# An mLSTM and Fourier-mixing kernel on Trainium2: first MLP weights by pairs of column blocks, and another order of VectorE's queue in the later batches

## The chip, the core and the metric

The kernel runs on one core of a Trainium2 chip. A core has TensorE (PE in the profile; PEld are its weight loads), VectorE (DVE), ScalarE (ACT), GpSimd (POOL) and SyncE (SP), each with an instruction queue that is worked off in order. Here SP's queue issues the transfers. The metric is the device time of one launch in microseconds.

## What is computed

Four batches, each of 768 tokens with 8 heads of 40 features, so 320 columns. First an mLSTM cell, then a block of Fourier mixing and an MLP:

```python
# mLSTM, per token t (the kernel works in chunks of 128 tokens instead)
C = f_stab * C + i_stab * outer(v_t, k_t);  n = f_stab * n + i_stab * k_t
y[t] = sigmoid(o_t) * (C @ q_t) / max(|n . q_t|, 1)

# Fourier mixing and MLP, x of shape (4, 768, 320)
mixed = real(fft(fft(x, axis=1), axis=2))
u = x + mixed
un = (u - mean(u)) / sqrt(var(u) + 1e-06)
out = u + relu(un @ w_ch1) @ w_ch2        # 320 -> 1280 -> 320
```

## The kernel before

**One order for everything.** No scheduler moves instructions. `at(slot, phase, fn, ...)` puts a call into a plan, and `run` executes the plan sorted by slot and, in a slot, by phase: EVAC 0, FILL 1, MAIN 2, FILL_PE 3, with fractions between. The order of these calls is the order of each engine's queue. Each batch has an mLSTM of six chunks, a mixing stage and 32 MLP slots: batches 0 to 3 have their MLP in slots 31 to 62, 63 to 94, 95 to 126 and 127 to 158. In the MLP slots of one batch the mLSTM and the mixing of the next are interleaved, so TensorE's queue alternates between the two. Slot 31 begins at 59.3 us, slot 51 at 124.0.

**mLSTM.** For each chunk TensorE makes scores (L465), VectorE multiplies them with the decay matrix W (L471), GpSimd masks W (`affine_select`, L443), scales q (qg, L431) and v (vw, L437) and decays the state (L455). L479 multiplies qg with the state, L486 multiplies W with v. VectorE divides (L544 to L550) and adds state updates (L515). GpSimd's L521 copies a small column.

**Mixing.** `mix_fold` (L606 to L618, mostly VectorE) folds pairs of token chunks. In batches 2 and 3 `mix_fold_again` (L635 to L645, VectorE and GpSimd) folds once more. Products into PSUM banks `pz` and `pu` follow. `mix_add` (L746 to L757) adds a chunk of `pu` to x on VectorE, in place, and takes mean and variance. For chunk c=3 it first copies a row within `pu` (L746) and clears another (L747). ScalarE centers (L765, `uc`), TensorE transposes (`mix_turn`, L772, into a bank `put`) and ScalarE copies the result to `uT` (L777). `ORDER` = (0, 5, 1, 4, 2, 3) is the order of the chunks. `mix_rstd` takes 1/sqrt of the variances of six chunks, a 128x6 tile: four steps L785 to L790 for a start value, and three Newton iterations of three steps, L792 to L794, all on VectorE.

**PSUM.** Four banks pm0 to pm3 serve the mixing and the MLP. In batches 2 and 3 the mixing has its banks written out: `MIX` (L593) gives `pu` the banks 3, 2, 2 for the pairs (0,5), (1,4), (2,3), and `put` the banks 3, 3, 3, 3, 2, 3 for the chunks of ORDER.

**MLP.** Batch 0 uses plain products: `mlp_in` (L836, with the 64 rows of the tail on L840) and `mlp_out` (L942). Batches 1 to 3 use a Strassen-Winograd form of seven products instead of eight. `mlp_block` computes two blocks of 128 hidden columns in four slots, five times: products L896, tails L901, copies of banks on ScalarE (L914, L918, L923), and `add` (L905) on VectorE, which adds a bank to a hidden block and so frees that bank. `mlp_out_pair` computes the output of two chunks in four slots, three times, over two banks x and y in turn: product L998, then `residual` (L948) on VectorE, which reads the bank before the next product may go into it. `hidden_sums` (L984, VectorE) forms the sums that the next pair needs.

**Weights.** `w_ch1` and `w_ch2` reach the kernel as 64-bit floats. A `Piece` of 128x640 numbers (640 KB) is loaded (`load`, SP), then `take` (VectorE, L344 and L346) splits off exponent and mantissa, `convert` (ScalarE, L351 and L352) turns them into floats, and `join` (VectorE, L358, L360, L364) puts the value together. There are five pieces for `w_ch1` and five for `w_ch2`, with two raw buffers between them. `w1_sb` holds rows 0 to 127 and 192 to 319 of `w_ch1`, each with all 1280 columns; `w1t_sb` holds the 64 rows between. `weight_sums` (L874) forms the sums of blocks of `w1_sb` for the Winograd form; the letters A11, A21, A12, A22 stand for row part and column block.

Of the kernel before, what the change touches and what calls it, by code (L numbers as in the profile page):

```python
# [10 lines left out]
FP = mybir.dt.float32  # L11
# [39 lines left out]
def kernel(  # L51
# [51 lines left out]
    h_first = const.tile([L, NP, 1], FP, name="h_first")  # L103
    w1_sb = const.tile([L, 2, DFF], FP, name="w1_sb")
    w1t_sb = const.tile([L, DFF // 2], FP, name="w1t_sb")
    w2_sb = const.tile([L, NFF, DM], FP, name="w2_sb")
# [33 lines left out]
    def gates(gp):  # L140
# [41 lines left out]
        mlstm_load(0, 2)  # L182
        w1_pieces[1].load()
        for t in hT_bufs + Cd_bufs:
# [135 lines left out]
    class Piece:  # L320
# [33 lines left out]
        def join(self):  # L354
# [7 lines left out]
            for d in self.dst:  # L362
# [3 lines left out]

    part = 2 * DM
    w1_pieces = [Piece([w1_sb[:, f // 2, f % 2 * part:(f % 2 + 1) * part]], w_ch1[:, f * part:(f + 1) * part])
                 for f in (0, 2, 1, 3)]
    w1_pieces.insert(2, Piece([w1t_sb], w_ch1[:, 4 * part:]))  # L370
    w2_flat = w_ch2.rearrange("p f m -> p (f m)")
# [407 lines left out]
    def mix_rstd(b):  # L779

        k = mixes[b]
        v = st_p.tile([L, NT], FP, name="v", tag="v")
        y = k.rstd = st_p.tile([L, NT], FP, name="rstd", tag="rstd")
        t = st_p.tile([L, NT], FP, name="t", tag="t")
        nc.vector.tensor_scalar(out=v, in0=k.u[:, :, DM + 1], scalar1=1e-6, scalar2=None, op0=OP.add)  # L785
        nc.vector.tensor_scalar(out=t.bitcast(U32), in0=v.bitcast(U32), scalar1=1, scalar2=None,
                                op0=OP.logical_shift_right)
        nc.vector.tensor_scalar(out=y.bitcast(U32), in0=t.bitcast(U32), scalar1=-1.0, scalar2=float(0x5F3759DF),
                                op0=OP.mult, op1=OP.add)
        nc.vector.tensor_scalar(out=v, in0=v, scalar1=-0.5, scalar2=None, op0=OP.mult)  # L790
        for _ in range(3):
            nc.vector.tensor_tensor(out=t, in0=y, in1=y, op=OP.mult)  # L792
            nc.vector.tensor_tensor(out=t, in0=t, in1=v, op=OP.mult)
            nc.vector.scalar_tensor_tensor(out=y, in0=t, scalar=1.5, in1=y, op0=OP.add, op1=OP.mult)  # L794

    def plan_mix(b, s0, x_done, s_feat, s_add, s_turn):
        for j in range(TG):
            p = TG - 1 - j
            at(x_done[j], FILL + 0.5, mix_fold, b, p)
            if b == 0:  # L800
                at((s0 - 4, s0 - 2, s0)[j], FILL_PE + 4, mix_seq, b, p, (0, 1))
                at((s0 - 2, s0 - 2, s0)[j], FILL_PE + 4, mix_tail, b, p)
            elif b == 1 or j == 0:
                if b > 1:
                    for step, slot in enumerate((x_done[0], x_done[-1] + 2, x_done[-1] + 6)):
                        at(slot, FILL + 0.55, mix_fold_again, b, step)
                at(s0, FILL_PE + 4, mix_seq, b, p, (0,))
                at(s0 + 1, FILL_PE + 4, mix_seq, b, p, (1,))
                at(s0 + 2, FILL_PE + 4, mix_tail, b, p)
# [5 lines left out]
        for c, a, t in zip(ORDER, s_add, s_turn):  # L815
            at(a, FILL, mix_add, b, c)
            at(t, FILL + 0.1, mix_center, b, c)
            at(t, FILL_PE + (5 if b == 0 or c in ORDER[:4] else -0.1), mix_turn, b, c)
            if b > 0:
                at(t, FILL_PE + 6, mix_turn_out, b, c)  # L820
            elif t < s_mlp:
                at(t + 1, FILL + 0.2, mix_turn_out, b, c)
            else:
                at(t + 1, EVAC, mix_turn_out, b, c)


    def mlp_in(b, gr, f):
# [6 lines left out]
        for i, ch in ((1, 1),) if f % 2 else ((0, 0), (0, 1), (1, 0)):  # L834
            f0 = (f // 2 * 2 + i) * L
            nc.tensor.matmul(k.pm[i], w1_sb[:, ch, f0:f0 + L], u[2 * ch], start=(ch == 0), stop=False)  # L836
        if f % 2:
            for i in range(2):
                r = slice(i * TAIL, (i + 1) * TAIL)
                nc.tensor.matmul(k.pm[i], w1t_sb[r, f // 2 * L:(f // 2 + 1) * L], u[1][r], start=False, stop=True)  # L840

# [17 lines left out]
    def weight_sums(n):  # L859

        w = w1_sb.rearrange("p c (n two t) -> p c two n t", two=2, t=L)
        if n == 0:
# [5 lines left out]
        def view(t):  # L868
            return t.rearrange("p (n t) -> p n t", t=L)

        S2, S3, S4 = (view(w1x[t]) for t in ("S2", "S3", "S4"))
        out, x, y, op = ((S3, w[:, 0, 0], w[:, 0, 1], OP.subtract), (w[:, 0, 1], w[:, 0, 1], w[:, 1, 1], OP.add),
                         (S2, w[:, 0, 1], w[:, 0, 0], OP.subtract), (S4, w[:, 1, 0], S2, OP.subtract))[n]
        nc.vector.tensor_tensor(out=out, in0=x, in1=y, op=op)  # L874
# [11 lines left out]
    def mlp_block(b, i, step):  # L886
# [5 lines left out]
        T2, T3, T4 = w1x["T"]  # L892
        A = {(r, ch): block(w1_sb[:, ch], f + r) for r in range(2) for ch in range(2)}

# [3 lines left out]
        def tails(gr, banks):  # L898
            for r, bank in enumerate(banks):
                rows = slice(r * TAIL, (r + 1) * TAIL)  # L900
                nc.tensor.matmul(bank, block(w1t_sb, i)[rows], mlp_u(gr, 1)[rows], start=False, stop=True,  # L901
                                 skip_group_check=True)
# [123 lines left out]
    def plan_mlp(b, s):  # L1026
# [19 lines left out]
        for n in range(TG) if b > 0 else ():  # L1046
            for step in range(4):
                at(s, MAIN, mlp_out_pair, b, n, step)
                if n < TG - 1 and step > 1:
                    for j in (2 * step - 3, 2 * step - 2):  # L1050
                        at(s, FILL + 0.3, hidden_sums, n + 1, (j,))
                s += 1
# [12 lines left out]
    def plan_batch(b, s_mlstm, s_mix, s_mlp):  # L1065
# [9 lines left out]
        else:  # L1075
            feat = [s_mix + c for c in ((3, 4, 6) if b == 1 else (3, 4, 7))]
            add = [s_mix + c for c in ((4, 4, 5, 6, 7, 7) if b == 1 else (4, 4, 5, 6, 8, 8))]
            turn = [s_mix + c for c in ((5, 6, 6) if b == 1 else (5, 6, 7))]
# [16 lines left out]

    when = [((2, 0.7), (4, 0.5), (6, 0.6)), ((6, 0.7), (7, 0.5), (8, 0.6)), ((11, 0.7), (13, 0.5), (22, 0.6))]
    when += [((22, 0.7), (23, 0.7), (27, 0.6)), ((27, 0.7), (28, 0.7), (32, 0.6))]
    when += [((s, 0.7), (s + 1, 0.7), (s + 2, 0.6)) for s in (33, 36, 39, 42, 45)]
    pieces = w1_pieces + w2_pieces
    for n, (w, p) in enumerate(zip(when, pieces)):  # L1100
        if n > 4:
            at(when[n - 2][2][0] + 1, FILL + 0.7, p.load)
        for (s, phase), fn in zip(w, (p.take, p.convert, p.join)):
            at(s, FILL + phase, fn)

    early = [(3, mlstm_load, 3), (3, mlstm_load_o, 2), (4, mlstm_load, 4), (5, mlstm_load_decay, 3),
             (5, mlstm_load_decay, 4), (6, None, 2), (7, mlstm_load_o, 3), (7, mlstm_load, 5),
             (11, mlstm_load_decay, 5), (11, None, 3), (11, mlstm_load_o, 4), (12, load_tables, None),
             (14, mlstm_load_o, 5), (23, None, 4)]
    for s, load, c in early:  # L1110
# [66 lines left out]
def _pack_w1(w):  # L1177

    t = w[L:L + TAIL].reshape(TAIL, NFF // 2, 2, L).transpose(2, 0, 1, 3).reshape(L, DFF // 2)
    return np.ascontiguousarray(np.concatenate([w[0:L], w[L + TAIL:], t], axis=1))  # L1180

# [45 lines left out]
```

## Time and profile before

The profiled execution took 431.76 us, of which the trace's span is 430.0 us. The median of 13 runs is 431.68 us (430.45 to 432.41).

| stretch, us | what runs | length | PE | DVE | ACT | POOL |
|---|---|---|---|---|---|---|
| 0 to 59.34 | gates, mLSTM and mixing of batch 0 | 59.34 | 53.86 | 49.53 | 39.71 | 25.36 |
| 59.34 to 124.0 | first MLP half of batch 0, mLSTM of batch 1 | 64.66 | 63.13 | 52.08 | 41.16 | 25.44 |
| 124.0 to 182.6 | second MLP half of batch 0, batch 1 | 58.60 | 58.60 | 38.13 | 20.94 | 16.96 |
| 182.6 to 225.5 | blocks of batch 1, mLSTM of batch 2 | 42.90 | 41.26 | 29.25 | 21.01 | 8.44 |
| 225.5 to 280.7 | output of batch 1, mixing of batch 2 | 55.20 | 53.18 | 39.72 | 22.42 | 18.14 |
| 280.7 to 322.5 | blocks of batch 2, mLSTM of batch 3 | 41.80 | 39.72 | 28.80 | 19.86 | 7.15 |
| 322.5 to 363.9 | output of batch 2, mixing of batch 3 | 41.40 | 39.82 | 26.80 | 8.39 | 0.00 |
| 363.9 to 397.5 | blocks of batch 3 | 33.60 | 32.69 | 15.00 | 14.71 | 0.00 |
| 397.5 to 430.0 | output of batch 3 | 32.50 | 29.06 | 16.66 | 1.35 | 0.00 |

The columns after the length are the busy time of each engine in microseconds. What a stretch could give at most is the length less TensorE's busy time, as long as TensorE's own work stays. A timeline row gives start, duration, engine, line, operation, output and inputs with their sizes and, in brackets, how long the engine was idle before it and whom it waited for.

### The profile page before, as it was taken

The numbers are of one execution on the slowest core, as the hardware profiler recorded it, in microseconds if no ns is written. First come the engines' busy times: TensorE is split into PE (matmuls) and PEld (weight loads), VectorE is DVE, ScalarE is ACT, GpSimd is POOL, SyncE is SP. The second block draws the span as 40 slices with busy tenths as digits, with TensorE's granted clock in tenths as the row PEclk, the third lists the DMA queues.
The fourth block names the chain that finished last, engine by engine and source line by source line (L and its number), as shares of the span: only waits on it lengthen the run. The fifth ranks groups of instructions, "written<-read, shape, count | busy, mean of one in ns | idle before, by whom it ended". The sixth has DMA issues, their size and how long they took to land.

```text
span 430.0 us, 7976 instructions
## 1 busy us (share of the span) xinstructions
PE 411.3 (96%) x2966; PEld 303.2 (70%) x2966; DVE 296.0 (69%) x718; ACT 189.5 (44%) x493; POOL 101.5 (24%) x146
## 2 busy tenths in 40 slices
PE   8999999999999999999999989999999999999997
PEld 6877555566667777866459888975449887454996
DVE  6799895779986456877756678578746774344752
ACT  6886376575651233654454322653451122344100
POOL 4654201464333322240101413440100000000000
DMA  7889296659454244366000534300000000000001
GB/s 215 253 238 345 78 282 238 199 195 274 155 164 142 81 125 143 114 200 184 2 1 2 178 114 133 120 18 0 0 2 0 33 30 22 10 0 2 15 36 42
DMA packets 20549, 47.14 MB, mean 110 GB/s; under 512 B 2784, under 2 KB 9312, under 8 KB 20384
## 3 DMA queue, kind: packets, MB, share of 16 engines
q1 hardware_dynamic: 20512, 46.65, 35.0%
q8 instruction: 23, 0.38, 0.4%
q14 instruction: 14, 0.11, 0.1%
HBM read 42.52 MB, written 4.11 MB: 108 GB/s over the span
## 4 chain that ended last, share of the span: by engine, by line
PE 73%; DVE 16%; issue 4%; ACT 3%; DMA 2%; POOL 1%; SPq 0%; DVEq 0%; ACTq 0%; POOLq 0%
PE po L998 17%; PE pm L896 14%; PE po L942 8%; PE ps L465 5%; PE ph L486 4%; PE pu L729 3%; PE ph L479 3%; PE pm L901 3%; PE pm L836 3%; PE px L535 2%; PE pz L698 2%; PE put L772 2%; DVE h L905 1%; DMA kvt<-in_kv 1%; PE pM L218 1%
## 5 line engine op out<-in xcount | busy, mean ns | idle before, releaser
L948 DVE SCALAR_TENSOR_TENSOR x<-po,rstd,x 128x160 f32<-128x160 f32 (+1 forms) x69 | 27.2, 395 | 37.9 <-PE po L998 31.4
L905 DVE TENSOR_TENSOR h<-h,pm 128x384 f32<-128x384 f32 x60 | 30.5, 549 | 32.7 <-ACT h L918 24.1
L421 ACT ACTIVATE W<-W,colT 128x128 f32<-128x128 f32 x144 | 45.1, 395 | 0.0
L443 POOL TENSOR_SCALAR_AFFINE_SELECT W<-W 128x1024 f32<-128x1024 f32 x18 | 22.1, 1228 | 97.0 <-ACT W L421 76.3
L896 PE MATMUL pm<-uT,w_sb 128*128 128x384 f32 x90 | 33.1, 495 | 3.6 <-DVE h L905 3.2
L777 ACT COPY uT<-put 128x384 f32<-128x384 f32 x24 | 11.3, 478 | 55.5 <-PE put L772 55.5
L942 PE MATMUL po<-w_sb,h 128*128 128x320 f32 x120 | 34.4, 435 | 0.0
L471 DVE TENSOR_TENSOR W<-ps,W 128x512 f32<-128x512 f32 x48 | 30.7, 681 | 2.9 <-POOL W L443 2.7
L836 PE MATMUL pm<-uT,w_sb 128*128 128x384 f32 x80 | 29.6, 499 | 0.7 <-DVE x L749 0.5
L998 PE MATMUL po<-T,S 128*128 128x160 f32 x180 | 27.8, 301 | 2.4 <-DVE x L948 2.4
L942 PEld LDWEIGHTS po<-w_sb,h 128*128 128x128 f32 x120 | 22.2, 190 | 9.5 <-issue 0.8
L998 PEld LDWEIGHTS po<-T,S 128*128 128x128 f32 x180 | 25.4, 190 | 4.4 <-DVE x L948 3.9
L465 PE MATMUL ps<-qk 40*128 40x128 f32 x384 | 28.1, 284 | 0.0
L998 PE MATMUL po<-w_sb,h 128*128 128x160 f32 x180 | 26.2, 301 | 1.1 <-DVE h L905 1.1
L998 PEld LDWEIGHTS po<-w_sb,h 128*128 128x128 f32 x180 | 24.9, 190 | 2.8 <-DVE h L905 2.4
L896 PEld LDWEIGHTS pm<-uT,w_sb 128*128 128x128 f32 x90 | 15.9, 189 | 15.3 <-DVE h L905 7.2
L465 PEld LDWEIGHTS ps<-qk 40*128 40x128 f32 x384 | 23.7, 187 | 4.2 <-issue 0.7
L486 PE MATMUL ph<-W,kvt 128*41 128x128 f32 x384 | 25.8, 277 | 0.0
L431 POOL TENSOR_TENSOR qg<-qk,Gb 128x512 f32<-128x512 f32 x18 | 25.0, 1391 | 0.7 <-DMA Gb<-G_d 0.6
L479 PEld LDWEIGHTS ph<-qg,C 128*128 128x128 f32 x160 | 20.0, 191 | 6.2 <-issue 1.9
L901 PE MATMUL pm<-uT,w1t_sb 64*128 64x384 f32 x120 | 24.1, 509 | 0.0
L935 ACT ACTIVATE h<-h 128x384 f32<-128x384 f32 x45 | 23.0, 524 | 1.5 <-DVE h L905 1.5
(206 smaller groups left out, 827.5 us busy)
## 6 DMA issues: line engine op xcount, KB each, us to landing
W<-M_d SPq DMA_DIRECT2D x18, 512.0 KB
kvt<-in_kv SPq DMA_DIRECT2D x24, 324.0 KB
qk<-in_qkT SPq DMA_DIRECT2D x48, 160.0 KB
raw<-in_w SPq DMA_DIRECT2D x10, 640.0 KB
Gb<-G_d SPq DMA_DIRECT2D x36, 128.0 KB
so<-in_o SPq DMA_DIRECT2D x24, 160.0 KB
out<-x SPq DMA_DIRECT2D x24, 160.0 KB
ds_sb<-in_dft_s SPq DMA_DIRECT2D x1, 1155.0 KB
```

The lines of the kernel that those rows point to most:

```text
L421: nc.scalar.activation(out=k.W[:, h, :], in_=M, func=AF.Exp, scale=-1.0, bias=colT[:, c, 0, b * H + h:b * H + h + 1])
L465: nc.tensor.matmul(k.ps[hip][:, p, :], k.qk[r, 1, p, :], k.qk[r, 0, p, :], start=True, stop=True)
L471: nc.vector.tensor_tensor(out=Wv, in0=k.ps[hip], in1=Wv, op=OP.mult)
L479: nc.tensor.matmul(k.ph[:, p, :], k.C[:, p, :], k.qg[:, p, :], start=(p == 0), stop=False, skip_group_check=True)
L486: nc.tensor.matmul(k.ph[hip * 64:hip * 64 + D1, p, :], k.v1[:, 2 * p + hip, :], k.W[:, 2 * p + hip, :], start=(c == 0 and p == 0), stop=Tr ...
L836: nc.tensor.matmul(k.pm[i], w1_sb[:, ch, f0:f0 + L], u[2 * ch], start=(ch == 0), stop=False)
L896: nc.tensor.matmul(bank, w, u, start=start, stop=True, skip_group_check=True)
L901: nc.tensor.matmul(bank, block(w1t_sb, i)[rows], mlp_u(gr, 1)[rows], start=False, stop=True, skip_group_check=True)
L905: nc.vector.tensor_tensor(out=h, in0=h, in1=bank, op=OP.add)
L942: nc.tensor.matmul(k.po, hidden(gr, f)[:, i * L:(i + 1) * L], w2_sb[:, f, :], start=(f == 0), stop=(f == NFF - 1))
L948: nc.vector.scalar_tensor_tensor(out=u, in0=po, scalar=k.rstd[:, c:c + 1], in1=u, op0=OP.mult, op1=OP.add)
L998: nc.tensor.matmul(po, a[:, f], w[:, f], start=start and f == 0, stop=f == half - 1, skip_group_check=True)
```

## The change

1. **Layout of `w_ch1`.** The host packs it so that one piece of 640 columns holds one pair of column blocks: A11, A21, A12, A22 and the tail block, 128 columns each. `w1_sb` becomes 128 x 5 x 5 x 128, `w1t_sb` goes, and `mlp_in`, `mlp_block` and `weight_sums` address it accordingly.
2. **Times of the conversions.** The list of ten (take, convert, join) loses the entry of slots 6 to 8 and gets one at slots 48 to 50. The pieces after the first come one entry later. One load leaves the opening part of the kernel, and the last one is issued at slot 45.
3. **Newton's iterations** in `mix_rstd` go from VectorE to GpSimd, as four instructions instead of three for each iteration.
4. **Phases of VectorE's work** in the mixing of batches 2 and 3: `mix_fold` and `mix_fold_again` go from FILL to FILL_PE (behind the slot's `mlp_block`), `mix_add` from FILL to MAIN + 0.5 (behind the slot's `mlp_out_pair`), and the last `mix_add` one slot later. For batches 1 to 3 `hidden_sums` of the next pair go from FILL + 0.3 to MAIN + 0.6.

```diff
@@ -101,8 +101,8 @@
     fe = const.tile([L, TG, 2 * PAD], FP, name="fe")
     fe_odd = const.tile([L, PAD], FP, name="fe_odd")
     h_first = const.tile([L, NP, 1], FP, name="h_first")
-    w1_sb = const.tile([L, 2, DFF], FP, name="w1_sb")
-    w1t_sb = const.tile([L, DFF // 2], FP, name="w1t_sb")
+
+    w1_sb = const.tile([L, NFF // 2, 5, L], FP, name="w1_sb")
     w2_sb = const.tile([L, NFF, DM], FP, name="w2_sb")
     uT_bufs = [const.tile([L, 3, TG, L], FP, name=f"uT{n}") for n in range(2)]
     NQ = 3
@@ -180,7 +180,6 @@
         w1_pieces[0].load()
         nc.sync.dma_start(out=spread_sb, in_=spread)
         mlstm_load(0, 2)
-        w1_pieces[1].load()
         for t in hT_bufs + Cd_bufs:
             nc.gpsimd.memset(t, 0.0)
 
@@ -364,10 +363,8 @@
                 nc.vector.tensor_tensor(out=d, in0=m[r], in1=self.e.bitcast(FP)[r], op=OP.mult)
                 at_ += d.shape[0]
 
-    part = 2 * DM
-    w1_pieces = [Piece([w1_sb[:, f // 2, f % 2 * part:(f % 2 + 1) * part]], w_ch1[:, f * part:(f + 1) * part])
-                 for f in (0, 2, 1, 3)]
-    w1_pieces.insert(2, Piece([w1t_sb], w_ch1[:, 4 * part:]))
+    w1_pieces = [Piece([w1_sb[:, i].rearrange("p k t -> p (k t)")], w_ch1[:, i * 5 * L:(i + 1) * 5 * L])
+                 for i in range(NFF // 2)]
     w2_flat = w_ch2.rearrange("p f m -> p (f m)")
     w2_pieces = [Piece([w2_sb[:, f:f + 2, :].rearrange("p f m -> p (f m)")], w2_flat[:, f * DM:(f + 2) * DM])
                  for f in range(0, NFF, 2)]
@@ -789,21 +786,22 @@
                                 op0=OP.mult, op1=OP.add)
         nc.vector.tensor_scalar(out=v, in0=v, scalar1=-0.5, scalar2=None, op0=OP.mult)
         for _ in range(3):
-            nc.vector.tensor_tensor(out=t, in0=y, in1=y, op=OP.mult)
-            nc.vector.tensor_tensor(out=t, in0=t, in1=v, op=OP.mult)
-            nc.vector.scalar_tensor_tensor(out=y, in0=t, scalar=1.5, in1=y, op0=OP.add, op1=OP.mult)
+            nc.gpsimd.tensor_tensor(out=t, in0=y, in1=y, op=OP.mult)
+            nc.gpsimd.tensor_tensor(out=t, in0=t, in1=v, op=OP.mult)
+            nc.gpsimd.tensor_scalar(out=t, in0=t, scalar1=1.5, scalar2=None, op0=OP.add)
+            nc.gpsimd.tensor_tensor(out=y, in0=t, in1=y, op=OP.mult)
 
     def plan_mix(b, s0, x_done, s_feat, s_add, s_turn):
         for j in range(TG):
             p = TG - 1 - j
-            at(x_done[j], FILL + 0.5, mix_fold, b, p)
+            at(x_done[j], FILL + 0.5 if b < 2 else FILL_PE + 0.2, mix_fold, b, p)
             if b == 0:
                 at((s0 - 4, s0 - 2, s0)[j], FILL_PE + 4, mix_seq, b, p, (0, 1))
                 at((s0 - 2, s0 - 2, s0)[j], FILL_PE + 4, mix_tail, b, p)
             elif b == 1 or j == 0:
                 if b > 1:
                     for step, slot in enumerate((x_done[0], x_done[-1] + 2, x_done[-1] + 6)):
-                        at(slot, FILL + 0.55, mix_fold_again, b, step)
+                        at(slot, FILL_PE + 0.25, mix_fold_again, b, step)
                 at(s0, FILL_PE + 4, mix_seq, b, p, (0,))
                 at(s0 + 1, FILL_PE + 4, mix_seq, b, p, (1,))
                 at(s0 + 2, FILL_PE + 4, mix_tail, b, p)
@@ -813,7 +811,7 @@
         for p in range(TG):
             at(s_feat[p], FILL_PE + 4, mix_feat, b, p)
         for c, a, t in zip(ORDER, s_add, s_turn):
-            at(a, FILL, mix_add, b, c)
+            at(a, FILL if b < 2 else MAIN + 0.5, mix_add, b, c)
             at(t, FILL + 0.1, mix_center, b, c)
             at(t, FILL_PE + (5 if b == 0 or c in ORDER[:4] else -0.1), mix_turn, b, c)
             if b > 0:
@@ -832,12 +830,11 @@
         if f % 2 == 0:
             k.pm = [bank("pm", [L, TG * L]) for _ in range(2)]
         for i, ch in ((1, 1),) if f % 2 else ((0, 0), (0, 1), (1, 0)):
-            f0 = (f // 2 * 2 + i) * L
-            nc.tensor.matmul(k.pm[i], w1_sb[:, ch, f0:f0 + L], u[2 * ch], start=(ch == 0), stop=False)
+            nc.tensor.matmul(k.pm[i], w1_sb[:, f // 2, 2 * ch + i], u[2 * ch], start=(ch == 0), stop=False)
         if f % 2:
             for i in range(2):
                 r = slice(i * TAIL, (i + 1) * TAIL)
-                nc.tensor.matmul(k.pm[i], w1t_sb[r, f // 2 * L:(f // 2 + 1) * L], u[1][r], start=False, stop=True)
+                nc.tensor.matmul(k.pm[i], w1_sb[r, f // 2, 4], u[1][r], start=False, stop=True)
 
 
     hid = {}
@@ -858,7 +855,7 @@
 
     def weight_sums(n):
 
-        w = w1_sb.rearrange("p c (n two t) -> p c two n t", two=2, t=L)
+        A11, A21, A12, A22 = (w1_sb[:, :, j] for j in range(4))
         if n == 0:
             x, y = (cp.tile([L, DM * 2], mybir.dt.int64, name="raw", tag="raw").bitcast(FP) for _ in range(2))
             w1x.update(S2=x[:, 0:DFF // 2], S3=x[:, DFF // 2:DFF], S4=y[:, 0:DFF // 2],
@@ -869,8 +866,8 @@
             return t.rearrange("p (n t) -> p n t", t=L)
 
         S2, S3, S4 = (view(w1x[t]) for t in ("S2", "S3", "S4"))
-        out, x, y, op = ((S3, w[:, 0, 0], w[:, 0, 1], OP.subtract), (w[:, 0, 1], w[:, 0, 1], w[:, 1, 1], OP.add),
-                         (S2, w[:, 0, 1], w[:, 0, 0], OP.subtract), (S4, w[:, 1, 0], S2, OP.subtract))[n]
+        out, x, y, op = ((S3, A11, A21, OP.subtract), (A21, A21, A22, OP.add), (S2, A21, A11, OP.subtract),
+                         (S4, A12, S2, OP.subtract))[n]
         nc.vector.tensor_tensor(out=out, in0=x, in1=y, op=op)
 
     def mlp_u(gr, ch):
@@ -890,7 +887,7 @@
         k = mixes[b]
         f = 2 * i
         T2, T3, T4 = w1x["T"]
-        A = {(r, ch): block(w1_sb[:, ch], f + r) for r in range(2) for ch in range(2)}
+        A = {(r, ch): w1_sb[:, i, 2 * ch + r] for r in range(2) for ch in range(2)}
 
         def product(bank, w, u, start=False):
             nc.tensor.matmul(bank, w, u, start=start, stop=True, skip_group_check=True)
@@ -898,7 +895,7 @@
         def tails(gr, banks):
             for r, bank in enumerate(banks):
                 rows = slice(r * TAIL, (r + 1) * TAIL)
-                nc.tensor.matmul(bank, block(w1t_sb, i)[rows], mlp_u(gr, 1)[rows], start=False, stop=True,
+                nc.tensor.matmul(bank, w1_sb[rows, i, 4], mlp_u(gr, 1)[rows], start=False, stop=True,
                                  skip_group_check=True)
 
         def add(h, bank):
@@ -1048,7 +1045,7 @@
                 at(s, MAIN, mlp_out_pair, b, n, step)
                 if n < TG - 1 and step > 1:
                     for j in (2 * step - 3, 2 * step - 2):
-                        at(s, FILL + 0.3, hidden_sums, n + 1, (j,))
+                        at(s, MAIN + 0.6, hidden_sums, n + 1, (j,))
                 s += 1
         for gr in groups if b == 0 else ():
             for i in range(TG):
@@ -1074,7 +1071,7 @@
             late = [s_mlp + 2, s_mlp + 5, s_mlp + 7]
         else:
             feat = [s_mix + c for c in ((3, 4, 6) if b == 1 else (3, 4, 7))]
-            add = [s_mix + c for c in ((4, 4, 5, 6, 7, 7) if b == 1 else (4, 4, 5, 6, 8, 8))]
+            add = [s_mix + c for c in ((4, 4, 5, 6, 7, 7) if b == 1 else (4, 4, 5, 6, 8, 9))]
             turn = [s_mix + c for c in ((5, 6, 6) if b == 1 else (5, 6, 7))]
             late = [s_mix + c for c in ((7, 8, 8) if b == 1 else (8, 9, 10))]
             at(s_mlp, EVAC + 0.5, mlp_sums)
@@ -1093,20 +1090,20 @@
 
     at(60, FILL + 0.4, lambda: nc.gpsimd.memset(ds_sb[0:1, 0, 0, :], 1.0))
 
-    when = [((2, 0.7), (4, 0.5), (6, 0.6)), ((6, 0.7), (7, 0.5), (8, 0.6)), ((11, 0.7), (13, 0.5), (22, 0.6))]
-    when += [((22, 0.7), (23, 0.7), (27, 0.6)), ((27, 0.7), (28, 0.7), (32, 0.6))]
-    when += [((s, 0.7), (s + 1, 0.7), (s + 2, 0.6)) for s in (33, 36, 39, 42, 45)]
+    when = [((2, 0.7), (4, 0.5), (6, 0.6)), ((11, 0.7), (13, 0.5), (22, 0.6)), ((22, 0.7), (23, 0.7), (27, 0.6)),
+            ((27, 0.7), (28, 0.7), (32, 0.6))]
+    when += [((s, 0.7), (s + 1, 0.7), (s + 2, 0.6)) for s in (33, 36, 39, 42, 45, 48)]
     pieces = w1_pieces + w2_pieces
     for n, (w, p) in enumerate(zip(when, pieces)):
-        if n > 4:
+        if n > 3:
             at(when[n - 2][2][0] + 1, FILL + 0.7, p.load)
         for (s, phase), fn in zip(w, (p.take, p.convert, p.join)):
             at(s, FILL + phase, fn)
 
     early = [(3, mlstm_load, 3), (3, mlstm_load_o, 2), (4, mlstm_load, 4), (5, mlstm_load_decay, 3),
-             (5, mlstm_load_decay, 4), (6, None, 2), (7, mlstm_load_o, 3), (7, mlstm_load, 5),
-             (11, mlstm_load_decay, 5), (11, None, 3), (11, mlstm_load_o, 4), (12, load_tables, None),
-             (14, mlstm_load_o, 5), (23, None, 4)]
+             (5, mlstm_load_decay, 4), (6, None, 1), (7, mlstm_load_o, 3), (7, mlstm_load, 5),
+             (11, mlstm_load_decay, 5), (11, None, 2), (11, mlstm_load_o, 4), (12, load_tables, None),
+             (14, mlstm_load_o, 5), (23, None, 3)]
     for s, load, c in early:
         at(s, FILL + 0.8, *((pieces[c].load,) if load is None else (load,) if c is None else (load, 0, c)))
 
@@ -1176,8 +1173,10 @@
 
 def _pack_w1(w):
 
-    t = w[L:L + TAIL].reshape(TAIL, NFF // 2, 2, L).transpose(2, 0, 1, 3).reshape(L, DFF // 2)
-    return np.ascontiguousarray(np.concatenate([w[0:L], w[L + TAIL:], t], axis=1))
+
+    t = w[L:L + TAIL].reshape(TAIL, NFF // 2, 2, L).transpose(2, 0, 1, 3).reshape(L, NFF // 2, L)
+    a, z = (r.reshape(L, NFF // 2, 2 * L) for r in (w[0:L], w[L + TAIL:]))
+    return np.ascontiguousarray(np.concatenate([a, z, t], axis=2).reshape(L, -1))
 
 
 def _pack_w2(w):
```

## The prediction, made before the changed kernel had run

> **What bounds the kernel now.** I read the busy shares first, then the chain that ended last, the list of waits for TensorE, and the timelines of VectorE and TensorE around each wait.
>
> ```profile
> PE 411.3 (96%) x2966; PEld 303.2 (70%) x2966; DVE 296.0 (69%) x718; ACT 189.5 (44%) x493; POOL 101.5 (24%) x146
> PE 73%; DVE 16%; issue 4%; ACT 3%; DMA 2%; POOL 1%; SPq 0%; DVEq 0%; ACTq 0%; POOLq 0%
> PE pm L896 <- DVE h L905: 3.2, 4, 0.8
> PE po L998 <- DVE x L948: 3.1, 4, 1.2
> ```
>
> TensorE (PE) is busy 411.3 of 430.0 us at a granted clock of 1.00 in every stretch I asked for, and its matmuls are the same before and after. So the change can only touch what TensorE waits for. The waits' columns are the sum, the times and the longest: eight waits on VectorE (DVE), 6.3 us, stand on the lines that the reordering touches (one of them, at 400.9, stays). They look like this in batch 1's blocks (VectorE, then TensorE; start and duration first):
>
> ```profile
> 191.68 0.49 DVE L606 TENSOR_TENSOR eo<-x 128x320 f32<-128x320 f32 x1
> ...
> 193.04 0.32 DVE L613 TENSOR_TENSOR fe<-eo 128x159 f32<-128x159 f32 x1
> 193.39 1.02 DVE L905 TENSOR_TENSOR h<-h,pm 128x384 f32<-128x384 f32 x2
> ```
>
> ```profile
> 192.28 0.91 PE L896 MATMUL pm<-m,w_sb 128*128 128x384 f32 x2
> 194.00 1.24 PE L896 MATMUL pm<-uT,w_sb 128*128 128x384 f32 x3 [0.81 <-DVE h L905]
> ```
>
> The fold L606-L613 (1.65 us) sits ahead of the three additions L905 that free the banks. The next block's second product normally starts .75 us after its first; here it starts 1.72 after: .97 lost.
>
> Elsewhere VectorE alone is full:
>
> ```profile
> 90.00:100.00 10.00, 10.00 (x81) 6.58 (x81) 9.42 (x26) 5.36 (x17) 5.56 (x9) 1.00 0.77 230
> 100.00:110.00 10.00, 10.00 (x84) 6.87 (x81) 9.69 (x18) 7.25 (x18) 5.39 (x6) 1.00 0.91 269
> ...
> 111.63 1.13 PE L479 MATMUL ph<-qg,C 128*128 128x128 f32 x8 [0.73 <-DVE den L544]
> ```
>
> The rows give length, then busy TensorE, its weight loads, VectorE, ScalarE, GpSimd (POOL), clock, DMA. VectorE has 9.4 and 9.7 us of work in 10, and TensorE stops for it at 111.63.
>
> **Part 1, additions before folds** (blocks of batches 1 to 3). Removed from the path: in batch 1 .97 at 192.3; .70 at 207.4 (the tails L901 take 2.19 instead of 1.49, the fold ahead of a single L905); 1.00 at 209.6 (Newton steps and L638 ahead of three L905), of which .3 stays, since four steps L785-L790 and a fold are still ahead of them. Sum 2.37. In batch 2 .98 at 290.6 and .93 at 307.3, of which .63 goes: 1.60. Batch 3 .26 at 382.9. What is late next are the folds themselves, 1.5 us later on VectorE; they feed products several slots on, so this costs nothing while the slots between are over 6 us.
>
> **Part 2, bank readings before mix_add and hidden_sums** (output stages). Two idle stretches go in the stage from 225.5, at 248 (1.32 as a gap between the products), and three in the stage from 322.6 (.12, .79 and 1.05: 1.96). The last looks like this:
>
> ```profile
> 356.35 1.62 PE L998 MATMUL po<-T,S 128*128 128x160 f32 x10 [0.88 <-DVE x L948]
> ```
>
> But the order gives something back. The last mix_add (c=3) now comes one slot later and behind the residual L948 of the y product, and it reads a bank (number 2) which the transposes L772 of c=2 fill next; they stand in TensorE's queue right behind that y product. In the trace before, this addition was long done. Now the transposes wait for the residual (.5 from the product's end), L746 and L747 (.62) and L751-L754 (1.0), with hand-over some 2.2 us. Behind them on TensorE stands all of the output stage. In the stage from 225.5 the transposes move from 272.06 to 272.06 - 1.32 - .42 (their own wait for ScalarE) + 2.2, some 272.2 to 272.5; in the other from 359.17 - 1.96 + 2.2 to about 359.4. I count -.15 for each: the 3.3 us gained are spent.
>
> **Part 3, Newton's steps to GpSimd.** Nine instructions of VectorE become twelve of GpSimd (multiply-add is split). In batch 0 VectorE spends this on them:
>
> ```profile
> 93.57 0.94 DVE L793 TENSOR_TENSOR t<-t,v 128x6 f32<-128x6 f32 x1
> 94.54 1.21 DVE L794 SCALAR_TENSOR_TENSOR rstd<-t,rstd 128x6 f32<-128x6 f32 x1
> ```
>
> From 92.77 to 96.27, 3.5 us for nine steps that take .2 each when alone. It is worth what TensorE loses to a late VectorE: .28 at 101.56 (the scores L465 take 1.44 instead of 1.16) and .90 at 111.63. Together 1.18.
>
> The price is on GpSimd, in whose queue the twelve go ahead of a copy L521, the mask L443 and the scaling of q L431:
>
> ```profile
> 93.38 1.11 POOL L443 TENSOR_SCALAR_AFFINE_SELECT W<-W 128x1024 f32<-128x1024 f32 x1 [0.95 <-DMA Gb<-G_d]
> 94.46 1.26 POOL L431 TENSOR_TENSOR qg<-qk,Gb 128x512 f32<-128x512 f32 x1
> ```
>
> No row shows GpSimd on 128x6. Near ones: a copy of 128x4 is .18, a 1x161 addition .51 (.59 start to start). From below, .25 with its gap; from above, 1.2, which a step of VectorE took while GpSimd ran beside it. I take .36, between the two near rows and closer to the small one: 4.3 us from 92.9 to 97.2. Then .2 + 1.1 + 1.3 bring qg to 99.9; the product L479 that reads it starts at 100.47. The limit is .41 per step.
>
> Here a rule of the Trainium skill speaks against the move (SBUF — State Buffer, "SBUF: two separate sides"): VectorE with two operands in SBUF and GpSimd reading SBUF share a port pair under an exclusive lock, and the loser blocks for the whole instruction. The weight joins L358, L360 and L364 (about .8 each) run just then. The row: GpSimd's vw L437 took 1.26 beside L358 and L360 at 79.76, .73 alone, so +.53, and GpSimd ends at about 100.5: no stall beyond .1. By the rule each join blocks a step, +2.4, qg at 102.3, a stall of 1.9. The trace's 1.21 for a step beside GpSimd leans to the rule, the other row against it; I take a stall of .6. Part 3 nets 1.2 - .6 = .6, from +1.2 to -.7 by rule and row; at 1.2 a step it would be -9. In batches 1 and 2 GpSimd idles (L639 waits up to 16.8 us) and L644 is met up to .85 a step; batch 3 has nothing else on it.
>
> **Part 4, the weights.** Same bytes, same five pieces of 640 KB, the same conversions; the matmuls still read 128 columns side by side, and L874 reads with another stride in the same count (.81 us each; ±0). One conversion leaves the first 30 us: there TensorE waits for ScalarE, not for this piece (±.2, taken 0). Its load leaves SP's queue at 8.7 us and one more is issued at slot 45, ahead of one so: SP has no busy time that the chain shows. The last piece of w2 is now converted at slots 48 to 50: .9 on VectorE at 119.4, two ScalarE steps (1.2), 2.4 at 122.4, while the last four of L942's first twenty matmuls (124.02 to 129.67) need it from 128.5, or 127.9 with part 3's gain. VectorE has 2.37 us idle before 129.71, and part 3 brings it forward; done at 124.8 to 127.3. I count 0; without that cover up to 1 us.
>
> **Sum.** .6 + 2.37 + 1.60 + .26 - .30 = 4.5 us off the profiled execution's 431.76 (span 430.0 and 1.76 around it), 427.3; the median 431.68 is .08 lower: **427.2**.
>
> **Rivals.** *More of it stays* (12%): the transposes' wait is shorter than 2.2, and GpSimd's steps hide. 4.5 + 3.3 + .6 = 8.4 at most, 423.3; I say 424. For: the chunk adds might be early. Against: the queue order is fixed. *Eaten* (13%): GpSimd's steps take .7; qg is 12 x (.7 - .41) = 3.5 late, net gain about 1.0 to 1.6: 430.3. For: 1.21 for L794. *The last w2 piece late* (6%): 1 to 2 us at 128, 428.5. *Slower* (11%): GpSimd's step price in batch 0. Each us of it costs 12; from about .77 a step (4.2 us late) all gain is gone, at .95 it is 434. For: every step reads SBUF on both sides of VectorE's joins. Against: the .18 row of a copy. My forecast has 58%, 425.6 to 429.3.
>
> **Numbers.** 0.2% (.86 us) is about what can be told from no change. Faster by more (under 430.8): the forecast, more, late w2 and half of eaten, .81; same .08; slower .11. The range, 425.0 to 430.2, leaves out most of the slower case and half of more.
>
> **What would show it.** Right: no waits of L896 on L905 at about 192, 209, 291 and 307; in each of the two output stages one L772 waiting some 2.2 us for VectorE; GpSimd steps of .3 to .4 with L479 within 1 us of 100; the first 59 us unchanged. Wrong: L772 without a wait (then 3 us more); GpSimd's steps near 1 us; L942 stopping near 128 for L364.

## The result, and the profile after

The changed kernel took 428.31 us (median of 11 runs, 426.75 to 429.81) beside 431.44 us for the kernel before (48 runs). The ratio is 0.9925 (95% interval 0.9909 to 0.9941): 3.2 us less, in which 2.5 to 3.9 are possible. In a second comparison it was 428.76 beside 430.60, ratio 0.9950 (0.9932 to 0.9969). The forecast was 427.2, the range 425.0 to 430.2.

Lines of the changed kernel stand three lower than those of before from the folds on: L893 is L896, L902 is L905, L945 is L948, L769 is L772, L476 is L479, L468 is L471. The page of the changed kernel (busy times, shares of the chain), and the list of TensorE's waits:

```profile
PE 408.5 (96%) x2966; PEld 301.9 (71%) x2966; DVE 288.7 (68%) x682; ACT 189.7 (45%) x493; POOL 115.1 (27%) x194
PE 76%; DVE 11%; DMA 5%; issue 3%; ACT 2%; POOL 2%; SPq 1%; POOLq 0%; ACTq 0%; DVEq 0%
```

```profile
PE put L769 <- DVE x L751: 4.3, 2, 2.1
...
PE ph L476 <- DVE den L541: 0.9, 1, 0.9
...
PE po L995 <- DVE x L945: 0.4, 1, 0.4
```

The waits on the additions (3.2 us before) are gone, and of the waits on the residuals 0.4 of 3.1 are left. In their place stand two waits of 2.1 us of the transposes, which the prediction had priced at 2.2. The stop of 0.9 at L476 is still there.

TensorE works off the same 2966 matmuls in the same order, so one can ask when the same matmul starts in both traces. The table gives the change in the length of each stretch, in us, between such starts; the second profile is that of the same kernel in the other comparison.

| stretch (times of before) | predicted | profile | second profile |
|---|---|---|---|
| 0 to 17.5, opening | 0 | -1.83 | -1.14 |
| 17.5 to 124.0, batch 0, mLSTM of batch 1 | -0.60 | +1.30 | +0.94 |
| 124.0 to 182.5 | 0 | 0.00 | 0.00 |
| 182.5 to 225.4, blocks of batch 1 | -2.37 | -2.66 | -2.67 |
| 225.4 to 280.7, output of batch 1 | +0.15 | +0.25 | +0.23 |
| 280.7 to 322.6, blocks of batch 2 | -1.60 | -1.88 | -1.89 |
| 322.6 to 363.9, output of batch 2 | +0.15 | +0.24 | +0.24 |
| 363.9 to 397.5, blocks of batch 3 | -0.26 | -0.37 | -0.37 |
| 397.5 to the end, output of batch 3 | 0 | +0.64 | +0.64 |
| sum | -4.5 | -4.3 | -4.0 |

The sums agree; the parts do not. Batch 0, with batch 1's mLSTM, lost 0.9 to 1.3 us instead of winning 0.6, and the opening gave what no part of the prediction had asked of it. The experiments take these apart.

### The profile page after: what moved, and what is told of

It reads as the page before. It is cut to its first block, busy times and chain, and to the rows that moved or that the text cites. A ratio compares the mean times of both kernels' runs of the same rounds, so it can differ in the third digit from the quotient of the medians.

```text
span 425.7 us, 7991 instructions
## 1 busy us (share of the span) xinstructions
PE 408.5 (96%) x2966; PEld 301.9 (71%) x2966; DVE 288.7 (68%) x682; ACT 189.7 (45%) x493; POOL 115.1 (27%) x194
## 4 chain that ended last, share of the span: by engine, by line
PE 76%; DVE 11%; DMA 5%; issue 3%; ACT 2%; POOL 2%; SPq 1%; POOLq 0%; ACTq 0%; DVEq 0%
PE po L995 18%; PE pm L893 17%; PE po L939 8%; PE ps L462 5%; PE pm L898 5%; PE ph L483 4%; PE pu L726 4%; PE ph L476 3%; DMA qk<-in_qkT 2%; PE px L532 2%; PE put L769 2%; PE pm L833 2%; DVE S L981 2%; PE pz L695 2%; DVE W L468 1%
## 5 line engine op out<-in xcount | busy, mean ns | idle before, releaser
L945 DVE SCALAR_TENSOR_TENSOR x<-po,rstd,x 128x160 f32<-128x160 f32 (+1 forms) x69 | 27.1, 395 | 42.1 <-PE po L995 37.9
L902 DVE TENSOR_TENSOR h<-h,pm 128x384 f32<-128x384 f32 x60 | 30.5, 550 | 33.4 <-ACT h L915 24.7
L440 POOL TENSOR_SCALAR_AFFINE_SELECT W<-W 128x1024 f32<-128x1024 f32 x18 | 21.8, 1211 | 93.3 <-ACT W L418 72.2
L468 DVE TENSOR_TENSOR W<-ps,W 128x512 f32<-128x512 f32 x48 | 30.7, 680 | 9.1 <-PE ps L462 4.7
L939 PE MATMUL po<-w_sb,h 128*128 128x320 f32 x120 | 34.4, 435 | 0.0
L893 PE MATMUL pm<-uT,w_sb 128*128 128x384 f32 x90 | 32.8, 492 | 0.2 <-DVE uT L881 0.2
L939 PEld LDWEIGHTS po<-w_sb,h 128*128 128x128 f32 x120 | 22.2, 190 | 9.5 <-issue 0.8
L789 POOL TENSOR_TENSOR t<-rstd 128x6 f32<-128x6 f32 x12 | 2.9, 244 | 91.9 <-DVE v L787 91.3
L428 POOL TENSOR_TENSOR qg<-qk,Gb 128x512 f32<-128x512 f32 x18 | 25.0, 1389 | 0.1
L476 PEld LDWEIGHTS ph<-qg,C 128*128 128x128 f32 x160 | 20.0, 191 | 6.6 <-issue 3.2
L893 PEld LDWEIGHTS pm<-uT,w_sb 128*128 128x128 f32 x90 | 16.2, 190 | 10.8 <-DVE h L902 1.5
```

Of the source, the lines that this page charges most:

```text
L428: nc.gpsimd.tensor_tensor(out=k.qg, in0=k.qk[:, 0], in1=k.Gb, op=OP.mult)
L468: nc.vector.tensor_tensor(out=Wv, in0=k.ps[hip], in1=Wv, op=OP.mult)
L476: nc.tensor.matmul(k.ph[:, p, :], k.C[:, p, :], k.qg[:, p, :], start=(p == 0), stop=False, skip_group_check=True)
L893: nc.tensor.matmul(bank, w, u, start=start, stop=True, skip_group_check=True)
L902: nc.vector.tensor_tensor(out=h, in0=h, in1=bank, op=OP.add)
L939: nc.tensor.matmul(k.po, hidden(gr, f)[:, i * L:(i + 1) * L], w2_sb[:, f, :], start=(f == 0), stop=(f == NFF - 1))
```

## The experiments

Each was timed beside the kernel before, and one execution of each was profiled.

### Is the opening's gain real? The changed kernel again

No edit.

> The changed kernel once more, as a second profile of it. If the 1.85 us that its first 17 us are shorter than before's come from the change, this profile shows them again (first wide pd product near 15.6 us instead of 17.5); if they are chance, it lies anywhere between. The time stays 2.5 to 4 us under before.

The first pd product (L296) started at 16.32 us, against 15.64 in the first profile and 17.48 in the trace of before. All later profiles, whatever the kernel, put it between 15.4 and 17.4; three kernels with the old loads and conversions in the opening (order_only, newton_only, old_weights) have it at 15.7, 16.7 and 15.4. TensorE's first rows show why. Before, then after:

```profile
4.98 0.28 PE L249 MATMUL pt<-ident,a 32*128 32x32 f32 x1 [0.79 <-DVE a L196]
5.20 0.61 PE L213 MATMUL pM<-later_b,ident_b 128*128 128x512 bf16 x1
5.60 1.91 PE L218 MATMUL pM<-M,ident 128*128 128x128 f32 x8
```

```profile
4.11 0.31 PE L248 MATMUL pt<-ident,a 32*128 32x32 f32 x1
4.35 0.60 PE L212 MATMUL pM<-later_b,ident_b 128*128 128x512 bf16 x1
4.75 1.09 PE L217 MATMUL pM<-M,ident 128*128 128x128 f32 x8
```

The eight products L218 take 1.91 us in one trace and 1.09 in the other. TensorE starts at half rate, and the moment when it comes to full rate differs from run to run: the clock changes in the traces have it at 4.2 us in newton_slot50, 6.0 here and 9.2 in bank3, and the first pd product then starts at 15.5, 16.3 and 17.4. In bank3 the same eight products take 1.91 us too. The opening's 1.1 to 1.8 us are thus a late start of the one profile of before, not a gain of the change: the gain that the two profiles show without it is 2.5 and 2.9 us.

A second part of the table varies by profile as well. Near 70 us take waits for a raw load (5.4 us in order_only, 5.6 here), and TensorE behind it loses 0 to 0.7 us against the trace of before, whatever parts of the change a kernel has: 0 in newton_only, 0.4 in order_only, 0.2 and 0.55 in the changed kernel's two profiles, 0.7 in bank3. It is no price of an early opening, since bank3 came there as late as before did. Without it the changed kernel lost 0.4 to 1.1 us in that stretch.

### One part at a time

order_only is the kernel before with item 4 of the change alone, newton_only with item 3 alone, weights_only with items 1 and 2 alone:

```diff
# order_only
-            at(x_done[j], FILL + 0.5, mix_fold, b, p)
+            at(x_done[j], FILL + 0.5 if b < 2 else FILL_PE + 0.2, mix_fold, b, p)
-                        at(slot, FILL + 0.55, mix_fold_again, b, step)
+                        at(slot, FILL_PE + 0.25, mix_fold_again, b, step)
-            at(a, FILL, mix_add, b, c)
+            at(a, FILL if b < 2 else MAIN + 0.5, mix_add, b, c)
-                        at(s, FILL + 0.3, hidden_sums, n + 1, (j,))
+                        at(s, MAIN + 0.6, hidden_sums, n + 1, (j,))
...
# newton_only
-            nc.vector.scalar_tensor_tensor(out=y, in0=t, scalar=1.5, in1=y, op0=OP.add, op1=OP.mult)
+            nc.gpsimd.tensor_scalar(out=t, in0=t, scalar1=1.5, scalar2=None, op0=OP.add)
+            nc.gpsimd.tensor_tensor(out=y, in0=t, in1=y, op=OP.mult)
...
# weights_only
-    when += [((s, 0.7), (s + 1, 0.7), (s + 2, 0.6)) for s in (33, 36, 39, 42, 45)]
+    when += [((s, 0.7), (s + 1, 0.7), (s + 2, 0.6)) for s in (33, 36, 39, 42, 45, 48)]
...
```

> The kernel before with the changed phases of mix_fold, mix_fold_again, mix_add and hidden_sums alone. Theory of the prediction: the block stages give 2.37 + 1.60, and what the output stages win is spent again at one transpose each, so 3.7 to 4.0 us less than before, with L772 waiting some 2.1 us twice. Rival 'more of it stays': 6 us or more less. Rival from the trace of after (early gain real, order worth less): under 3 us less.

> The kernel before with the Newton steps on GpSimd alone, in all four batches. Theory of the prediction: 0.6 us less in batch 0 and, since two folds stay ahead of L905, another 0.7 at most in batch 1; together 0.6 to 1.3 us less. Rival, read from the trace of after: the steps delay GpSimd's mask in batch 0, VectorE then waits for the mask, and TensorE stops at 110 as before: 0 to 0.5 us less (batch 1 alone).

> The changed kernel with the order of VectorE's queue and the Newton steps as before, so that the weights' layout and the times of their conversion are alone. Theory of the prediction: 0 (from -0.4 to +0.4). Rival A, the trace of after read as it stands: the first 17 us are 1.85 shorter because one load and one conversion less stand in the opening, and the conversion at slot 48 costs 0.85 at 120 us, so 1.0 less than before. Rival B: the 1.85 us are chance (the first wait for in_i), and the late conversion costs 0.85: 0.8 more than before.

| kernel | ratio to before (interval) | 17.5 to 124 | blocks 1 | blocks 2 | blocks 3 |
|---|---|---|---|---|---|
| order_only | 1.0057 (1.0038 to 1.0076) | +0.41 | +0.76 | -0.15 | -0.01 |
| newton_only | 0.9959 (0.9940 to 0.9977) | +0.07 | -1.11 | -1.03 | -0.38 |
| weights_only | 1.0023 (1.0010 to 1.0037) | +0.93 | -0.01 | +0.38 | 0.00 |

order_only missed its expectations, newton_only won more than expected (1.8 us by the ratio) and elsewhere; weights_only came out as its rival B. The order alone made the kernel **slower**, by 2.5 us. Its VectorE, then its TensorE, in the blocks of batch 1:

```profile
204.60 0.49 DVE L606 TENSOR_TENSOR eo<-x 128x320 f32<-128x320 f32 x1
...
206.19 0.16 DVE L785 TENSOR_SCALAR v<-x 128x6 f32<-128x6 f32 x1
...
208.40 0.17 DVE L794 SCALAR_TENSOR_TENSOR rstd<-t,rstd 128x6 f32<-128x6 f32 x1
208.48 1.48 DVE L905 TENSOR_TENSOR h<-h,pm 128x384 f32<-128x384 f32 x3
```

```profile
206.48 0.91 PE L896 MATMUL pm<-m,w_sb 128*128 128x384 f32 x2
209.08 3.84 PE L896 MATMUL pm<-uT,w_sb 128*128 128x384 f32 x6 [1.69 <-DVE h L905]
```

The fold, moved behind one addition, now stands together with all thirteen steps of mix_rstd ahead of the next three additions: 208.48 minus 204.60 is 3.9 us, and TensorE waits 1.69 instead of 0.83. So the two parts help each other. In the blocks of batches 1 and 2 the Newton move alone gives 2.1, the order alone 1.1 (its 0.76 holds 1.7 of another cause, shown next), both together 4.5. In the row above there is a second thing: six matmuls take 3.84 us, where newton_only's take 2.10. The stretches of order_only around the wait of its transposes (length, busy time of TensorE, weight loads, VectorE, ScalarE, GpSimd, granted clock, DMA):

```profile
357.00:359.00 2.00, 0.13 (x1) 0.16 (x2) 1.83 (x8) 0.00 (x0) 0.00 (x0) 1.00 0.00 0
359.00:360.00 1.00, 1.00 (x8) 1.00 (x8) 0.44 (x2) 0.57 (x2) 0.00 (x0) 0.84 0.00 0
360.00:361.00 1.00, 1.00 (x6) 1.00 (x5) 0.00 (x0) 0.42 (x1) 0.00 (x0) 0.50 0.00 0
...
363.00:364.00 1.00, 1.00 (x9) 1.00 (x9) 0.17 (x1) 0.00 (x0) 0.00 (x0) 0.96 0.00 0
```

Behind the wait the clock is 0.50 for 3.4 us (359.68 to 363.09), and the same behind the wait at 209. Each costs 1.7 us, as the stretch from the transposes to batch 3's first block shows: 6.44 us (358.87 to 365.31) instead of 4.76 in the changed kernel. Without these 3.4 us the order alone would be about even with the kernel before: its trace has it 1.1 us shorter in the blocks and 1.1 longer in the outputs. The changed kernel's two profiles had the same waits of 2.1 us and no such stretch. But six of its 22 timed runs show a mean clock of 0.995 or 0.996, which is what one stretch of 3.4 us at half clock makes of 427, and these six took 429.2 to 430.4 us where the others took 426.8 to 429.1.

newton_only won 2.5 us in its trace, all in the blocks, and nothing in batch 0. weights_only lost 0.64 at 120 us. Its VectorE, and its scores at 120:

```profile
117.60 0.49 DVE L343 TENSOR_SCALAR e<-raw 128x640 uint32<-128x640 uint32 x1
118.01 1.50 DVE L345 TENSOR_SCALAR m<-raw 128x640 uint32<-128x640 uint32 x1
119.54 1.29 DVE L468 TENSOR_TENSOR W<-ps,W 128x512 f32<-128x512 f32 x2
```

```profile
120.28 1.75 PE L462 MATMUL ps<-qk 40*128 40x128 f32 x16
```

take of the added piece stands ahead of L468, which empties the banks for the next scores. They take 1.75 us instead of 1.16.

### Taking the new waits away

Three edits of the changed kernel, alone and together:

```diff
# bank3
-    MIX = {"z": (2, 3), "zt": 2, "u": (3, 2, 2), "ut": (3, 3, 3, 3, 2, 3)}
+    MIX = {"z": (2, 3), "zt": 2, "u": (3, 2, 2), "ut": (3, 3, 3, 3, 3, 3)}
# late_take
-    when += [((s, 0.7), (s + 1, 0.7), (s + 2, 0.6)) for s in (33, 36, 39, 42, 45, 48)]
+    when += [((s, 0.7), (s + 1, 0.7), (s + 2, 0.6)) for s in (33, 36, 39, 42, 45)]
+    when += [((49, 0.3), (50, 0.2), (51, 0.2))]
# newton_slot50
-        at(s_mlp + NFF, FILL + 0.6, mix_rstd, b)
+        at(s_mlp + NFF + (9 if b == 0 else 0), FILL + 0.6, mix_rstd, b)
```

> The changed kernel with the transposes of c=2 in bank 3 instead of bank 2, so that they do not wait for the last mix_add, which reads bank 2. Theory (the wait of 2.1 us in each of two output stages is a bank's, and nothing else is late behind it): the two waits of L769 on L751 go and 3.6 to 4.2 us less than the changed kernel's 428.5, so 424.3 to 425. Rival (the wait is taken over by the transposes of c=3, which need the same chunk add and then ScalarE): under 2 us less.

> The changed kernel with the last piece's steps at slots 49 to 51, take behind the two L468 of slot 49 instead of ahead. Theory (the stall of the scores at 120.8, 0.24 + 0.59 us, comes from take ahead of L468): 0.6 to 0.9 less than the changed kernel. Rival (the piece then ends too late for the last four matmuls of the first output column): the stall moves to L939 near 127, 0 to 1 us more.

> The changed kernel with mix_rstd of batch 0 at slot 50 instead of 41, so that its GpSimd steps no longer stand ahead of the mask and the scaling of q at 91 to 97 us. Theory (that delay makes VectorE wait 1.5 us for the mask, which keeps the stop of L476 at 110): 0.3 to 1.2 less than the changed kernel, with the wait of 0.91 at 110 shorter or gone. Rival (the stop at 110 comes from the length of the joins beside GpSimd, L359 and L363 with 1.7 each): 0 to 0.2 less.

> The changed kernel with the three edits together: bank 3 for c=2, take of the last piece behind L468, mix_rstd of batch 0 at slot 50. If they are independent, the sum of the three: 4.5 to 6.3 us less than the changed kernel, 422.5 to 424; if they share a limit, not less than the best of them.

**bank3**: 425.18 us, ratio 0.9850 (0.9825 to 0.9874). The two output stages are 1.6 and 1.7 us shorter than in the changed kernel, a little short of the 3.6 expected of both and less than the two waits of 2.1, since c=3's transposes now wait 0.4 for ScalarE:

```profile
352.67 0.51 PE L769 MATMUL put<-ident,uc 128*128 128x128 f32 x3
...
356.32 0.55 PE L769 MATMUL put<-ident,uc 128*128 128x128 f32 x3 [0.42 <-ACT uc L762]
```

So the wait was the shared bank's, not the data's: the new order's gain in these stages had been given back to one bank number. They are now 1.4 us shorter each than before the change.

**late_take**: 427.85 us, ratio 0.9932 (0.9909 to 0.9956), which the interval cannot tell from the changed kernel's 0.9925 and 0.9950. The trace can: the scores take 1.16 again (121.81 to 122.97), where the changed kernel's two profiles lose 0.9 and 0.6 us, and L939 runs its first twenty matmuls in 5.65 us without a stop, as before.

**newton_slot50**: 427.14 us, ratio 0.9901 (0.9875 to 0.9927). From 17.5 to 124 us it takes 1.6 to 2.0 less than the changed kernel's two profiles. The stop at 110 is gone. In the changed kernel GpSimd and VectorE had looked like this:

```profile
91.16 0.78 POOL L789 TENSOR_TENSOR t<-rstd 128x6 f32<-128x6 f32 x1 [0.52 <-DVE v L787]
92.02 0.66 POOL L790 TENSOR_TENSOR t<-t,v 128x6 f32<-128x6 f32 x1
92.77 0.81 POOL L791 TENSOR_SCALAR t<-t 128x6 f32<-128x6 f32 x1
93.66 0.20 POOL L792 TENSOR_TENSOR rstd<-t,rstd 128x6 f32<-128x6 f32 x1
...
96.74 1.09 POOL L440 TENSOR_SCALAR_AFFINE_SELECT W<-W 128x1024 f32<-128x1024 f32 x1
```

```profile
97.86 1.29 DVE L468 TENSOR_TENSOR W<-ps,W 128x512 f32<-128x512 f32 x2 [1.53 <-POOL W L440]
```

VectorE, freed of the steps, waits 1.53 us for the mask, which stands behind the same steps on GpSimd. Two of the joins behind it then come beside GpSimd's next mask and scaling (L440 at 101.02, L428 at 102.57) and take twice as long. VectorE in the changed kernel, then newton_slot50:

```profile
101.57 1.71 DVE L359 SCALAR_TENSOR_TENSOR m<-raw,m 128x640 f32<-128x640 uint32 x1
103.31 1.78 DVE L363 TENSOR_TENSOR w_sb<-m,e 128x640 f32<-128x640 f32 x1
```

```profile
96.48 1.29 DVE L468 TENSOR_TENSOR W<-ps,W 128x512 f32<-128x512 f32 x2
...
99.98 0.82 DVE L359 SCALAR_TENSOR_TENSOR m<-raw,m 128x640 f32<-128x640 uint32 x1
100.83 0.82 DVE L363 TENSOR_TENSOR w_sb<-m,e 128x640 f32<-128x640 f32 x1
```

With the steps at slot 50 both are gone: L468 starts 1.4 us earlier without a wait, and the joins end at 101.65, when the next mask (101.20) has just begun. So the steps in this place of GpSimd's queue kept the stop at 110. The long joins, the rival of the expectation, are a part of it; what share is theirs and what the mask's, this edit doesn't tell. VectorE also reaches L468 at 120 early enough that take no longer costs there. The profile has one half-clock stretch (1.6 us) behind the transposes' wait at 267, and five of the six runs have a mean clock of 0.995 or 0.996, so the median understates the edit.

**all_three**: 422.57 us (422.31 to 423.08), ratio 0.9797 (0.9773 to 0.9820). The first stretch gains no more than with newton_slot50 alone: late_take and newton_slot50 cure the same wait.

### Where is half the clock lost, and what else is left?

```diff
# long_wait, on the changed kernel
-                nc.vector.memset(Q[0:1], 0.0)
+                for _ in range(9):
+                    nc.vector.memset(Q[0:1], 0.0)
# sums_first, on all_three
-                        at(s, MAIN + 0.6, hidden_sums, n + 1, (j,))
+                        at(s, FILL + 0.3 if b == 3 else MAIN + 0.6, hidden_sums, n + 1, (j,))
```

old_weights is all_three without items 1 and 2 of the change.

> The changed kernel with the memset of c=3 in mix_add issued nine times instead of once (batches 1 to 3), so that the transposes of c=2 wait some 1.6 to 1.9 us longer in each of the two output stages. Theory (TensorE's clock is halved for 3.4 us when it was idle for more than about half of such a stretch): the granted clock falls to 0.5 behind each of the two waits in the profile, each costing some 1.7 us beside the wait: 428.5 + 3.6 + 3.4 = 435 to 436. Rival (the half clock seen in two earlier profiles was chance): 428.5 + 3.6 = 432, with no stretch at half clock there.

> The kernel all_three with hidden_sums of batch 3 back at FILL + 0.3 (ahead of the slot's residuals). Theory (the 0.22 and 0.21 us that the changed kernel loses at two changes of pair in batch 3's output come from four sums standing together behind the residuals): 0.4 to 0.6 less than all_three, 422.0. Rival: the same as all_three.

> The kernel all_three with the layout of the first weights and all times of conversion as before the change. Theory (the weights' part brings nothing, and with take behind L468 costs nothing): within 0.5 us of all_three's 422.6. Rival A (one load and one conversion less in the opening are worth something): 0.5 to 1.5 us more. Rival B (the late piece still costs on VectorE at 120 to 128 us): 0.5 to 1 us less.

**long_wait**: 438.16 us, over the 435 to 436 of the theory and far over the rival's 432. Both waits are now 4.4 us, 2.3 longer where 1.6 to 1.9 were expected, and the clock falls behind both: from 271.85 to 278.67, two stretches, and from 364.01 to 367.42.

```profile
268.00:272.80 4.80, 0.45 (x4) 0.21 (x2) 3.39 (x16) 0.82 (x2) 3.43 (x5) 0.90 0.22 53
272.80:275.00 2.20, 2.13 (x9) 2.16 (x10) 1.80 (x4) 0.99 (x2) 0.00 (x0) 0.50 0.01 3
275.00:278.00 3.00, 3.00 (x13) 3.00 (x12) 0.38 (x1) 0.00 (x0) 0.00 (x0) 0.50 0.02 5
```

The two output stages are 5.1 and 4.0 us longer than in the changed kernel's profile; 2.3 of each is the wait, 2.8 and 1.7 are the half clock. Another 1.6 us are lost at 183 to 188 us, in batch 1's blocks, where the edit delays VectorE as well and TensorE waits 1.0 at L476.

**sums_first**: 421.59 us, ratio 0.9778 (0.9745 to 0.9811). The output of batch 3 is 0.64 us shorter, as short as before the change. **old_weights**: 422.31 us, ratio 0.9795 (0.9761 to 0.9828), the same as all_three within the intervals. Within these intervals, some 1.4 us each way, the weights' part brings nothing here and costs nothing once VectorE is ahead. sums_first has the lowest median, 9.4 us under the kernel before; the intervals of the last three overlap.

## Why the prediction was right, and where it was not

- **The time and the sign held; part of that is luck.** Two wrong terms of opposite sign cancel: the opening (0 predicted, -1.1 to -1.8 in the traces, all of it the late start of the one trace on which the sum was built) and batch 0 (-0.6 predicted, +0.9 to +1.3, of which 0.2 and 0.55 the chance wait at 70). Without the opening the gain is 2.5 to 2.9 us in the traces, where 4.5 had been forecast.
- **Part 1, blocks: mechanism right, size a little small, and wrongly credited.** 2.66, 1.88 and 0.37 for 2.37, 1.60 and 0.26: the 0.3 us that four steps and a fold were to keep did not stay. But "additions before folds" got credit for what Newton's move brought: newton_only alone won 1.11, 1.03 and 0.38 in the three stages, order_only, without its half clock, 0.9, 0.15 and 0.01. The prediction had put that move at 0.6, all of it in batch 0, where it won nothing.
- **Part 2, output stages: right.** The return of the gain at the transposes of c=2 was priced at 2.2 us and measured 2.13 twice; bank3 shows the cause. What was missed: the wait can halve the clock behind it, and hidden_sums behind the residuals cost 0.64 us in batch 3's output, which the sum had at nothing.
- **Part 3, Newton's steps: the step that failed is the gain, not the price.** The twelve steps took 5.5 us where 4.3 and some blocking had been taken, and L476 waited 0.24 us for qg, less than the 0.6 charged. The 0.28 at 101.56 came back, but the 0.90 us at 111.6 did not: I freed VectorE without asking what it would wait for next. It was the mask, whose delay on GpSimd I had priced for TensorE alone, and two joins that came late behind it took twice as long beside the next mask.
- **Part 4, weights: the step that failed is "I count 0" for the late piece.** I checked join against the last matmuls of L942 (right: these never waited) and not take against L471 in the same queue. The cost is 0.64 us at 120 in weights_only, and 0.9 and 0.6 in the changed kernel's two profiles; another 0.38 in weights_only's blocks of batch 2 is one longer wait for L901 at 291.7, whose cause stays open.
- **The rule weighed in part 3 was nearer than the row.** Three steps beside the three joins took 0.78, 0.66 and 0.81 us, those behind them 0.19 to 0.23 but for one of 0.73: each join blocked one step, as the Trainium skill has it (SBUF — State Buffer, "SBUF: two separate sides"). These three added 1.65 us, below the 2.4 worked out from the rule and above the row's 0.5. The one of 0.73 ran beside take (L343, L345), which neither working had counted.

## What to carry to other kernels

When work leaves a full engine, name what that engine waits for next and which queue now holds the work; a producer in the receiving queue can turn the whole gain into a wait. Put two changes to one queue on trial together and apart: here the order alone cost time, most of it through the half clock behind the waits that it left, and both together won. Before a stage's gain is written off as spent at a new wait, look at which resource the wait is for; if it is a bank number, it can be changed.

## What the hardware showed that was not expected

**A wait of TensorE of about 2 us can cost 1.7 us more.** The half-clock stretches last 3.41 us (6.83 once), and their starts lie on a grid of that length: in order_only 209.49 and 359.68 lie 44 such lengths apart, and the first lies 60 behind the change to full clock at 4.69. Counting TensorE's busy time in the piece of the grid ahead of each: 0.51 and 0.38 (order_only), 0.39 (newton_slot50), 0.01 and 0.18 (long_wait) where the clock fell, and 0.54 to 0.58 in the changed kernel's two profiles, where it did not. But a piece of 0.51 in order_only (at 305) and two of 0.49 and 0.45 in newton_slot50 kept the clock, so the border lies somewhere from 0.4 to a little over one half; busy ends are modelled, and it cannot be told closer. Whether a wait of about 2 us costs the clock thus depends on how it falls on the grid. To come back may take more: in long_wait the first piece at half clock was 0.70 busy and a second one followed. The Trainium skill (TensorE: Matmul & The Clock Gate, "HAM oscillation — how this bites in real kernels") warns of idle gaps over some 3.4 us; here waits of 1.69 and 2.13 were enough.

**The opening alone can differ by 2 us between profiles of kernels that are the same up to there.** That is more than half of what this change brought, and the granted clock does not show it: the stretches of the trace of before give 1.00 for the very time in which eight products took 1.91 instead of 1.09 us. That trace holds no clock change at all, and the other traces' records begin with the first change to full clock; so the prediction's 1.00 in every stretch was not measured there. Comparing starts of the same matmul behind the opening removes it.
